# Moving the next batch's attention one step ahead in the odd batches of a fused attention and gated MLP

## Chip, cores and metric

The kernel runs on one core of one Trainium2 chip. The metric is the device time of one execution in microseconds (us). TensorE, VectorE, ScalarE, GpSimd and SyncE appear in the profile as PE (with PEld for weight loads), DVE, ACT, POOL and SP.

## The reference, cut to what matters

```python
def _attn_ref(x, state):                    # x (8, 8, 512, 64), state (8, 8, 32, 64)
    a = softmax(scale * x @ state.T)        # 512 tokens attend to 32 states
    xread = a @ state
    a2 = softmax(scale * state @ x.T)       # and the states to the tokens
    sread = a2 @ x
    return concatenate([xread, sread], axis=2)

def _moe_ref(x, w_in, w_out):               # 4352 x 512, 512 x 2048, 2048 x 512
    h = x @ w_in
    g = h * np.cos(h)
    return g @ w_out
```

(`softmax` stands for the max, exp, sum and division that the reference writes out.)

## The kernel before

Each of the 8 batches is 16 steps. A step makes one 128 x 512 tile of `h`, gates it (h cos h, with range reduction), and multiplies an older tile into the output. Between these, the attention of the *next* batch is dealt out to the steps. Batches are taken in pairs; in odd batches 3 and 5 steps 0 to 7 make `h` by a scheme with fewer products, and steps 8 to 15 by plain matmuls:

```python
hps = ctx.enter_context(tc.tile_pool(name="hps", bufs=2, space=PSUM))   # two banks for h

def hidden(t):                                   # PE, L471
    t.hp = hps.tile([P, S], F32, name="h")[:, 0:t.n]
    for i in range(t.kn):
        nc.tensor.matmul(out=t.hp, lhsT=t.lhs(i), rhs=t.rhs(i), ...)
def gate(t):   nc.scalar.activation(t.q.bitcast(I32), t.hp, func=ACTF.Copy, bias=0.25)      # L567
def gate2(t):  nc.vector.tensor_tensor(t.q, t.q.bitcast(I32), t.hp, op=ALU.subtract)        # L570
def gate3(t):  nc.scalar.activation(t.q, t.q, func=ACTF.Sin, bias=halfpi, scale=-TWO_PI)    # L573
def gate4(t):  nc.vector.tensor_tensor(t.g, t.hp, t.q, op=ALU.mult)     # L580: h's bank is free
```

(some lines of these functions are cut). The order of one step, which is the order of each engine's queue:

```python
    # ... matmuls of h
    go(0)                       # attention's matmuls of this step
    gate(t); gate2(t)           # in odd steps 0-7, gate was made in the step before
    go(1); go(3)                # x_act, x_dve: attention's ops AHEAD of gate3 and gate4
    gate3(t)
    if later: later.pop(0)()    # a sum or an output transpose (store, L651) on VectorE
    gate4(t)
    sums(t)                     # "minus", L586
    go(2); go(4)                # y_act, y_dve: attention's ops BEHIND gate4
    # ... output matmuls (L624), of a tile three steps back
```

And the plan of the attention of batch `b + 1`, with `s` the list of steps 1, 2, 5, 6, 7, 8, 9:

```python
            pe[s[2]].append((b, "scores"))
            x_dve[s[2]].append((b, "max1"))         # L333
            x_dve[s[3]].append((b, "spread1"))      # L339: into rows of xT
            y_dve[s[3]].append((b, "shift"))        # L356
            x_dve[s[4]].append((b, "max2"))         # L349
            y_act[s[4]].append((b, "exps"))         # exp1 and exp2, with a table load
            x_dve[s[5]].append((b, "sums"))         # L333, L375, L376
            y_dve[s[5]].append((b, "spread1"))      # the second spread
            x_dve[s[6]].append((b, "norm1"))        # L386: aT = z1 * spread
```

The turned weights are copied (L397, twice in step 10), and read by L409 from step 11 on.

```python
            self.spread, self.z2 = xT[:, 0:2], xT[:, 2:4]
            self.a2T = xT[:, 0:2].rearrange("p j (c m) -> p j c m", c=NC)
```

Of the kernel before, what the change touches and what calls it, by code (L numbers as in the profile page):

```python
# [21 lines left out]
def kernel(  # L22
# [813 lines left out]
    def plan(b):  # L836
        pe, x_act, y_act, x_dve, y_dve = [
            {s: [] for s in range(NF)} for _ in range(5)]

        def prod(s, b, nt, *bank):  # L840
            pe[s].append((b, "products", nt) + bank)
            if b == 1 and 0 < nt < 3:
                x_dve[s].append((b, "products_taken", nt) + bank)
            else:
                x_act[s].append((b, "products_kept", nt) + bank)

        def pairs(s, b, name, kept, i):
            pe[s] += [(b, name, i), (b, name, i + 1)]
            x_act[s].append((b, kept, i))
            y_act[s].append((b, kept, i + 1))  # L850

        def early(b, s):
            if b == 1:
                pairs(s[0], b, "tokens", "tokens_kept", 0)
                pairs(s[1], b, "tokens", "tokens_kept", 2)
            else:
                for k in range(NK):
                    to = (x_dve, y_dve)[k % 2]
                    to[s[k // 2]].append((b, "tokens_turned", k))
            pe[s[2]].append((b, "scores"))  # L860
            x_dve[s[2]].append((b, "max1"))
            x_dve[s[3]].append((b, "spread1"))
            y_dve[s[3]].append((b, "shift"))
            x_dve[s[4]].append((b, "max2"))
            y_act[s[4]].append((b, "exps"))
            x_dve[s[5]].append((b, "sums"))
            y_dve[s[5]].append((b, "spread1"))
            x_dve[s[6]].append((b, "norm1"))

        def late(b, s):  # L870
            pairs(s[0], b, "turn", "turn_kept", 0)
            pe[s[1]].append((b, "reads", 0))
            pe[s[2]].append((b, "reads", 1))
            x_dve[s[2]].append((b, "keep"))
            if len(s) > 3:
                turned(b, s[3])

        def turned(b, s):
            pe[s].append((b, "keep2"))
            x_act[s].append((b, "keep3"))  # L880


        if b == 0:
            pe[0].append((0, "products", 0, SIDE, HC, WC))
            y_dve[0] += [(0, "products_taken", 0, SIDE, HC, WC),
                         (0, "inverse2")]
            prod(7, 0, 2, SIDE)
            prod(11, 0, 3)
            prod(13, 1, 0, MAIN)
            late(0, (1, 2, 3, 4))  # L890
            early(1, (5, 6, 7, 8, 9, 10, 11))
            late(1, (12, 13, 14))
        else:
            bank = (SIDE,) if b == 1 else ()
            if b == 1:
                turned(1, 0)
            prod(0, b, 1, *[MAIN for _ in bank])
            prod(4, b, 2, *bank)
            prod(9, b, 3, *bank)
            if b + 1 < B:  # L900
                prod(13, b + 1, 0)
                early(b + 1, (1 + (b == 1), 2 + (b == 1), 5, 6, 7, 8, 9))
                late(b + 1, (10, 11, 12, 15))
        return pe, x_act, y_act, x_dve, y_dve

# [21 lines left out]
    for step, t in enumerate(all_tiles):  # L927
        s = step % NF
        if s == 0 and t.b < B:
            steps = plan(t.b)  # L930
# [119 lines left out]
```

## Time and profile before

| | before |
|---|---|
| median | 765.45 us of 3 runs (764.82 to 768.66); 765.67 of 6, the 3 made beside the changed kernel included |
| span of the profiled run | 764.2 us |
| PE busy | 751.7 us, 98% |
| PE's waits for DVE's L580 | 4.3 us in all |
| late starts of L471 in steps 10 and 11 | 0.35 and 0.95 us, in batches 3 and 5 |
| granted clock, mean | 0.997 |

TensorE is as good as always busy, so time moves only where it waits. The lines are in the prediction. A line of the order of time reads: start, duration, engine, line of the kernel, operation, what it writes and reads, shape, count, and in brackets the idle time before it and what ended that. A tile's two matmuls make four records here, 0.43 us apart.

### The profile page before, as it was taken

The page shows a single profiled execution, that of the slowest core. Times are in us where ns is not written, and L with a number is a line of the kernel's source. Part 1 is how long each engine was busy: PE and PEld are TensorE (multiplying, and loading weights), DVE is VectorE, ACT ScalarE, POOL GpSimd, SP SyncE. Part 2 cuts the span into 40 slices and gives each one's busy share as a digit, 9 for nine tenths or more (in the row PEclk, how much of TensorE's full clock was granted, in tenths as well). Part 3 has the DMA queues.
Part 4 walks back from the last instruction along what each step waited for, and adds up shares of the span by engine and source line. Part 5 has one row for each costly group of instructions (what it writes and reads, how often), then busy time and mean ns, then how long its engine had stood idle before and what let it go on. Part 6 is the DMA issues. An engine that isn't in the chain of part 4 may idle for free.

```text
span 764.2 us, 8416 instructions
## 1 busy us (share of the span) xinstructions
PE 751.7 (98%) x2880; PEld 380.4 (50%) x2880; DVE 520.3 (68%) x862; ACT 316.3 (41%) x523; POOL 249.3 (33%) x258
## 2 busy tenths in 40 slices
PE   8998999999999999999999999999999999999997
PEld 3443443445555554445555553445555554455554
DVE  5778777836896788847886789747878676432431
ACT  3887844533254335333362335333443333212212
POOL 2354278777121210662221111751211206500200
PEclk9999999999999999999999999999999999999999
DMA  8595461050002510340105210420100115000021
GB/s 247 170 274 209 131 98 29 4 107 1 14 15 49 90 28 4 54 82 0 29 1 97 41 28 15 70 54 1 27 1 1 28 28 138 0 0 15 14 42 41
DMA packets 161962, 43.54 MB, mean 57 GB/s; under 512 B 153920, under 2 KB 153920, under 8 KB 161920
## 3 DMA queue, kind: packets, MB, share of 16 engines
q1 hardware_dynamic: 161024, 42.49, 25.7%
q10 hardware_dynamic: 768, 0.39, 0.2%
q8 instruction: 23, 0.38, 0.2%
q14 instruction: 19, 0.16, 0.1%
q0 software_dynamic: 128, 0.13, 0.1%
HBM read 34.08 MB, written 8.91 MB: 56 GB/s over the span
## 4 chain that ended last, share of the span: by engine, by line
PE 87%; DVE 7%; ACT 2%; issue 1%; DMA 1%; POOL 1%; SPq 0%; DVEq 0%; ACTq 0%; POOLq 0%
PE o L624 47%; PE h L514 14%; PE h L471 14%; PE at L319 4%; PE o L744 4%; PE at L409 2%; DVE xT L339 1%; PE o L319 1%; DVE q L570 1%; DVE g_all L580 1%; DVE i L333 1%; DMA g_all<-in_moe_w_in_dram 1%; ACT q L567 1%; PE at L392 1%; DVE aT L356 1%
## 5 line engine op out<-in xcount | busy, mean ns | idle before, releaser
L624 PE MATMUL o<-g_all,w_out 128*128 128x512 f32 x512 | 236.4, 598 | 0.4 <-POOL w_out L242 0.4
L624 PE MATMUL o<-g_all,s 128*128 128x512 f32 x384 | 177.3, 598 | 0.0
L586 POOL TENSOR_TENSOR g_all<-g_all 128x512 f32<-128x512 f32 x80 | 112.8, 1433 | 121.2 <-DVE g_all L580 121.2
L624 PEld LDWEIGHTS o<-g_all,w_out 128*128 128x128 f32 x512 | 93.8, 190 | 113.1 <-issue 108.4
L573 ACT ACTIVATE q<-q,halfpi 128x512 f32<-128x512 f32 (+1 forms) x144 | 100.8, 700 | 95.8 <-DVE q L570 95.6
L624 PEld LDWEIGHTS o<-g_all,s 128*128 128x128 f32 x384 | 70.8, 190 | 88.1 <-issue 82.1
L570 DVE TENSOR_TENSOR q<-q,h 128x512 f32<-128x512 int32 (+1 forms) x69 | 42.9, 621 | 103.6 <-ACT q L567 103.6
L471 PE MATMUL h<-aT,sw 128*128 128x512 f32 x224 | 107.2, 602 | 4.8 <-DVE g_all L580 4.3
L567 ACT ACTIVATE q<-g_all 128x512 int32<-128x512 f32 x75 | 46.8, 624 | 141.8 <-DVE g_all L560 141.4
L567 ACT ACTIVATE q<-h 128x512 int32<-128x512 f32 (+1 forms) x69 | 37.6, 545 | 131.0 <-PE h L471 131.0
L570 DVE TENSOR_TENSOR q<-q,g_all 128x512 f32<-128x512 int32 x75 | 52.7, 703 | 35.5 <-ACT q L567 35.5
L471 PEld LDWEIGHTS h<-aT,sw 128*128 128x128 f32 x224 | 41.8, 190 | 60.2 <-issue 45.0
L509 POOL TENSOR_TENSOR swS<-sw 128x128 f32<-128x128 f32 x35 | 17.4, 496 | 148.6 <-PE h L514 107.3
L580 DVE TENSOR_TENSOR g_all<-g_all,q 128x512 f32<-128x512 f32 x75 | 54.0, 720 | 14.5 <-ACT q L573 14.4
L580 DVE TENSOR_TENSOR g_all<-h,q 128x512 f32<-128x512 f32 (+1 forms) x69 | 42.8, 621 | 23.5 <-ACT q L573 23.1
L242 POOL TENSOR_TENSOR w_out<-w_out,s 128x1024 int32<-128x1024 int32 x10 | 23.9, 2390 | 77.6 <-DVE w_out L237 73.4
L509 POOL TENSOR_TENSOR swS<-sw,swS 128x128 f32<-128x128 f32 x35 | 18.3, 522 | 87.4 <-PE h L514 86.9
L514 PEld LDWEIGHTS h<-aT,sw 128*128 128x128 f32 x144 | 27.4, 190 | 34.4 <-issue 28.0
L514 PE MATMUL h<-aS,sw 128*128 128x256 f32 x144 | 43.1, 381 | 0.1
L514 PE MATMUL h<-aS,swS 128*128 128x256 f32 x144 | 42.8, 379 | 0.0
L514 PE MATMUL h<-aT,sw 128*128 128x256 f32 x144 | 42.8, 379 | 0.0
L586 DVE TENSOR_TENSOR g_all<-g_all 128x512 f32<-128x512 f32 x48 | 33.5, 697 | 1.6
(107 smaller groups left out, 886.3 us busy)
## 6 DMA issues: line engine op xcount, KB each, us to landing
out_dram<-ot SPq DMA_DIRECT2D x132, 64.0 KB, 2.0
g_all<-in_moe_w_out_dram SPq DMA_DIRECT2D x8, 1024.0 KB, 5.0
g_all<-in_moe_w_in_dram SPq DMA_DIRECT2D x6, 1024.0 KB, 5.3
xT<-in_x_dram SPq DMA_DIRECT2D x96, 64.0 KB, 2.3
x_b<-in_x_dram SPq DMA_DIRECT2D x24, 256.0 KB, 4.5
x_b<-in_x_dram SPq DMA_DIRECT2D x16, 128.0 KB, 3.8
g_all<-in_moe_w_in_dram SPq DMA_DIRECT2D x4, 512.0 KB, 5.9
x_b<-in_moe_w_out_dram SPq DMA_DIRECT2D x1, 1024.0 KB, 6.1
```

Of the source, the lines that this page charges most:

```text
L242: nc.gpsimd.tensor_tensor(bits, bits, e, op=ALU.add)
L319: nc.tensor.matmul(out=(to or at)[j][Ns * k:Ns * k + Ns, 0:n], lhsT=w[D * j:D * j + D, self.b, Ns * k:Ns * k + Ns], rhs=r(slice(D * j, D * ...
L471: nc.tensor.matmul(out=t.hp, lhsT=t.lhs(i), rhs=t.rhs(i), start=(i == 0), stop=(i == t.kn - 1))
L509: engine.tensor_tensor(o, x1, x2, op=op)
L514: nc.tensor.matmul(out=out, lhsT=w, rhs=r, start=True, stop=True)
L567: nc.scalar.activation(t.q.bitcast(I32), t.hp, func=ACTF.Copy, bias=0.25)
L570: nc.vector.tensor_tensor(t.q, t.q.bitcast(I32), t.hp, op=ALU.subtract)
L573: nc.scalar.activation(t.q, t.q, func=ACTF.Sin, bias=halfpi, scale=-TWO_PI)
L580: nc.vector.tensor_tensor(t.g, t.hp, t.q, op=ALU.mult)
L586: engine.tensor_tensor(out, a, b, op=ALU.subtract)
L624: nc.tensor.matmul(out=acc[bank][ch], lhsT=w[:, i, P * ch:P * ch + P], rhs=g.g, start=(i == 0), stop=(i == NH - 1))
L744: nc.tensor.matmul(out=acc[MAIN][i], lhsT=t.g[:, P * i:P * i + P], rhs=w_out[:, :, t.f, :], start=(t.n_th == 0), stop=(t.n_th == NF - 1))
```

## The change

Its intent is to take the next batch's attention out of steps 8 and 9, where TensorE's steps are short and VectorE's long, by doing it a step sooner. The small product (`prod`) has to leave step 4, whose two PSUM banks the scores now take.

```diff
-            prod(4, b, 2, *bank)
+
+            soon = int(b % 2 == 1 and b > 1)
+            prod(4 - soon, b, 2, *bank)
             prod(9, b, 3, *bank)
             if b + 1 < B:
                 prod(13, b + 1, 0)
-                early(b + 1, (1 + (b == 1), 2 + (b == 1), 5, 6, 7, 8, 9))
+                early(b + 1, (1 + (b == 1), 2 + (b == 1)) + tuple(
+                    s - soon for s in (5, 6, 7, 8, 9)))
                 late(b + 1, (10, 11, 12, 15))
```

## The prediction

> **What bounds the kernel now.** I read the page first, then TensorE's waits, then the order of time on each engine around the two places where TensorE waits in batch 3.
>
> ```profile
> PE 751.7 (98%) x2880; PEld 380.4 (50%) x2880; DVE 520.3 (68%) x862; ACT 316.3 (41%) x523; POOL 249.3 (33%) x258
> ...
> PE h L471 <- DVE g_all L580: 4.3, 6, 1.9
> ```
>
> TensorE is busy 751.7 of 764.2 us. Whatever the change does, it pays only through TensorE's waits, and most of what it still waits for in mid-kernel is the last gating multiply on VectorE (L580), which frees one of the two PSUM banks `h`. TensorE in order of time, batch 3, steps 8 to 11:
>
> ```profile
> 296.52 1.88 PE L471 MATMUL h<-aT,sw 128*128 128x512 f32 x4
> 298.24 1.88 PE L624 MATMUL o<-g_all,s 128*128 128x512 f32 x4
> 299.95 1.88 PE L471 MATMUL h<-aT,sw 128*128 128x512 f32 x4
> 301.76 1.09 PE L319 MATMUL at<-w_in,st_all 64*32 64x512 f32 x16
> 302.78 1.98 PE L624 MATMUL o<-g_all,s 128*128 128x512 f32 x4
> 304.95 1.98 PE L471 MATMUL h<-aT,sw 128*128 128x512 f32 x4 [0.18 <-DVE g_all L580]
> 306.77 1.04 PE L392 MATMUL at<-ident,xT 128*128 128x128 f32 x8
> 307.65 1.88 PE L624 MATMUL o<-g_all,s 128*128 128x512 f32 x4
> 310.32 1.98 PE L471 MATMUL h<-aT,sw 128*128 128x512 f32 x4 [0.79 <-DVE g_all L580]
> ```
>
> L471 opens steps 8, 9, 10 and 11. Matmul ends are modelled, so I use starts: step 8 without a wait is 299.95 - 296.52 = 3.43 us. A set of small products costs 1.22 more: even step 4 with it runs from 277.75 to 283.70, 5.95 us, and the same step 6 without it from 288.36 to 293.09, 4.73. So step 10 was due at 299.95 + 3.43 + 1.22 = 304.60 and came 0.35 late. Step 11 was due at 306.77 + 0.88 (turn) + 1.72 (output) = 309.37 and came 0.95 late. Batch 5 repeats both (472.24 and 477.61). All that the change can win is therefore 2 x (0.35 + 0.95) = 2.6 us, 0.34%.
>
> VectorE over the same stretch:
>
> ```profile
> 297.56 0.69 DVE L580 TENSOR_TENSOR g_all<-g_all,q 128x512 f32<-128x512 f32 x1
> 298.28 0.69 DVE L586 TENSOR_TENSOR g_all<-g_all 128x512 f32<-128x512 f32 x1
> 298.89 1.28 DVE L630 SCALAR_TENSOR_TENSOR held<-o,held 128x512 f32<-128x512 f32 x2
> 301.23 0.69 DVE L570 TENSOR_TENSOR q<-q,h 128x512 f32<-128x512 int32 x1 [1.06 <-ACT q L567]
> 301.83 1.30 DVE L333 TRANSPOSE_TENSOR_REDUCE i<-aT 128x16 f32<-128x512 f32 x2
> ...
> 304.25 0.65 DVE L580 TENSOR_TENSOR g_all<-h,q 128x512 f32<-128x512 f32 x1
> ...
> 305.54 1.24 DVE L339 STREAM_TRANSPOSE xT<-i 128x1024 f32<-128x1024 f32 x1
> ...
> 307.27 1.79 DVE L386 TENSOR_TENSOR aT<-aT,xT 128x1024 f32<-128x1024 f32 x1
> ```
>
> L580 at 304.25 is step 8's, and step 10's matmul starts 0.70 us after it. Before it stand step 8's sums (L333); *behind* it stand the spread (L339) and norm (L386) of the next batch. The 1.06 us of idle is ScalarE's: it does the exponentials from 297.02 to 300.60, both table loads around them, and takes step 8's first gate op only then.
>
> **What the Trainium skill says.** "TensorE: Matmul & The Clock Gate", Architectural detail, says ACT and DVE are "strict FIFO"; every order seen here agrees, so the order of the program decides. "ScalarE: Activation LUTs", What ACT_TABLE_LOAD costs, gives about 1283 ns a load; the loads at 297.02 and 301.21 took 1.28 us each. "GPSIMD Engine Reference", Specifications, says POOL shares SBUF interfaces with VectorE when an instruction has two SBUF inputs; L386 has a median of 1231 ns over its eight runs but took 1.79 us at 307.27, with POOL at work. The same TensorE page, Part 1, says that a free-running window of about 3.4 us with an idle array halves the clock for the next. The trace has one case: TensorE idle 1.95 us before 73.03, then
>
> ```profile
> 71.00:73.00 2.00, 0.09 (x1) 0.00 (x0) 1.95 (x3) 1.99 (x5) 0.48 (x1) 1.00 0.05 19
> 73.00:76.00 3.00, 2.97 (x4) 0.84 (x4) 1.90 (x3) 2.97 (x5) 1.87 (x1) 0.62 0.77 245
> ```
>
> (granted clock 0.62, third column from the end). Against the usual spacing the starts after 73.57 lost 0.29 + 0.42 + 0.47 + 0.40 = 1.6 us, about half of one window. The 0.95 waits did not trigger it (1.00).
>
> **The change, part by part.** No instruction is added or removed; it all lies in the order of queues. In batches 3 and 5 scores and max go from step 5 to 4, spread and shift to 5, max2 and exponentials to 6, sums and second spread to 7, norm to 8; the small product goes from step 4 to 3 (in batch 7 that alone, which I count as 0: the two copies behind it fit where ScalarE idles).
>
> TensorE does the same sum of work. Step 4 starts 1.22 later (278.97), step 5 too, step 6 as before at 288.36. I replay the in-order queues from there with the durations of the trace, start to start where ops stand back to back.
>
> Names: gate is ScalarE's L567, gate2 L570, sine L573, gate4 L580, minus L586; max L333, spread L339, shift L356, max2 L349 (with L351), sums L333 to L376, norm L386, store L651. In an even step L559 and L560 come first and gate waits for L560.
>
> - Step 4, VectorE: L560 at 278.97 + 1.49 = 280.46 (the same delay as at 259.97), gate2 1.45 later (281.91; that chain through ScalarE is as at 279.85 to 281.28). Then 0.61 gate2, 1.23 max, 0.62 store, 0.68 gate4, 0.61 minus: 285.66.
> - Step 5: gate2 0.61, wait 0.1, three adds 1.58, spread 1.16, gate4 0.69, minus 0.61, shift 1.20: 291.6. TensorE needs the adds by 288.36 and they end at 288.0.
> - Step 6: two adds to L560 at 292.0; gate2 at 293.45; 0.61, max2 1.40, gate4 0.70, minus 0.61: 296.8. ScalarE: sine 294.15, step 7's gate 294.8 to 295.4, then the exponentials with their table 295.4 to 299.0, then the sine table to 300.3.
> - Step 7: gate2 to 297.4; sums wait for exp1 (297.75) and end 299.6; gate4 waits for the sine, now *behind* the exponentials (300.35 to 301.07), so VectorE idles 1.4 and gate4 starts at 301.1. Then 0.72, minus 0.61, spread 1.16, L630 1.20: 304.8.
> - Step 8: gate2 0.61, norm 1.22 (POOL is idle there), store 0.65: gate4 at 307.3, against 304.25.
>
> So step 8's gate4 has spread and norm, 1.16 + 1.22 us, in front of it that stood behind it, and ScalarE's idle is not saved but moved a step earlier and is longer (1.4 for 1.06). Step 10's matmuls start at 307.3 + 0.70 = 308.0, 3.4 late instead of 0.35. Step 9's gate4 then comes at about 310.1, so step 11 no longer waits: 308.0 + 4.42 (step 10's length, 309.37 - 304.95) = 312.4, against 310.32. Loss 2.1 us a batch. Later steps have next to no waits that could take it back. Two batches: 4.2 us.
>
> Then the clock. An idle of 3.4 us leaves at least 1.6 us in one window wherever the window falls; here, if windows fall as now, about 2.2 us from 305.8. I put 0.85 on a halved window, at 1.65 us each: 2 x 0.85 x 1.65 = 2.8 us.
>
> Sum: 765.45 + 4.2 + 2.8 = 772.4.
>
> **Rivals.** (a) It works as meant: exponentials off step 8 let its gate op start 1.7 us sooner, and both waits go. For it: the 1.06 of VectorE idle before 301.23. Against: from 285 to 299 VectorE has hardly any idle, so it can't absorb work earlier. This makes 762.9 at best. (b) The waits only change places, with VectorE's total work before step 9's gate4 being the same in both: about 765 to 766. Against: the output of steps 8 to 10 is short (1.72 us), so a late step 10 leaves no room before step 11. (c) The loss without the clock: 769.7, if neither batch crosses into half rate. (d) Another wait, step 6's for step 5's adds (0.3 us of room): up to 1 us a batch more.
>
> **Range and chances.** (c) to (d) with both halvings span 769.7 to 775; an error of a microsecond a batch in the replay, or a run of before that is itself 0.5 high, opens the low side to 767. The range is 767.0 to 775.0. Faster by over 2% is impossible by the 2.6 us limit; slower by 2% would need 15 us.
>
> **What would show it.** Right: gate4 of step 8 near 307 with L339 and L386 ahead of it; an idle of some 3 us before L471 near 308 and 477, no wait before the next; a VectorE idle of over 1 us before the gate4 near 301, behind the table load; a window with granted clock under 1 after each wait. Wrong: gate4 of step 8 before 305, a total of TensorE waits below that of before, or a wait in steps 5 to 7 in place of step 10.

## The result and the profile after

The changed kernel took 772.53 us, median of 6 runs (771.24 to 773.3), against 765.67 for the kernel before. The ratio is 1.0083, 95% interval 1.0064 to 1.0103: slower by 0.8%, clear of noise. Ratios and intervals here are from fast runs of the same rounds; they are not quite the ratio of the medians. All outputs are right.

The page's line of busy times and the largest of TensorE's waits, kernel after:

```profile
PE 754.4 (98%) x2880; PEld 382.3 (50%) x2880; DVE 520.0 (67%) x862; ACT 317.2 (41%) x523; POOL 248.1 (32%) x258
...
PE h L471 <- DVE g_all L580: 8.5, 4, 3.1
```

TensorE's waits for L580 have doubled in sum, from 4.3 to 8.5 us, in 4 places instead of 6. Those that the change was to shorten, in batches 3 and 5, went from 2 x (0.18 + 0.79) = 1.9 to 2 x 3.08 = 6.2. TensorE in order of time, steps 8 to 11 of batch 3:

```profile
296.80 1.88 PE L471 MATMUL h<-aT,sw 128*128 128x512 f32 x4
...
303.06 1.98 PE L624 MATMUL o<-g_all,s 128*128 128x512 f32 x4
308.12 3.07 PE L471 MATMUL h<-aT,sw 128*128 128x512 f32 x4 [3.08 <-DVE g_all L580]
310.99 1.68 PE L392 MATMUL at<-ident,xT 128*128 128x128 f32 x8
312.51 1.88 PE L624 MATMUL o<-g_all,s 128*128 128x512 f32 x4
314.23 1.88 PE L471 MATMUL h<-aT,sw 128*128 128x512 f32 x4
```

Step 8 starts at 296.80, 0.28 later than before, which comes from the first microseconds of the run. Step 10 was due at 296.80 + 8.08 = 304.88 and starts 3.24 late. Step 11 then has no wait, but step 10 took 308.12 to 314.23, 6.11 us instead of 4.42: the L471 group shows why, 3.07 us for what took 1.98 before. In these traces the granted clock changes only at borders that lie a multiple of 3.413 us apart; one such stretch is called a window here. Two windows (columns: busy time and count of PE, PEld, DVE, ACT, POOL; then clock, DMA share, GB/s):

```profile
308.88:312.29 3.41, 3.41 (x10) 1.87 (x9) 2.99 (x5) 1.52 (x3) 3.41 (x3) 0.50 0.68 108
479.55:482.96 3.41, 3.41 (x9) 1.76 (x8) 2.83 (x6) 1.32 (x2) 3.41 (x3) 0.50 0.68 107
```

Both are at 0.50, the first in batch 3 and the second in batch 5, and each follows the window that holds most of the wait. VectorE shows where step 8's gate4 went:

```profile
301.40 0.69 DVE L580 TENSOR_TENSOR g_all<-g_all,q 128x512 f32<-128x512 f32 x1 [1.38 <-ACT q L573]
302.13 0.69 DVE L586 TENSOR_TENSOR g_all<-g_all 128x512 f32<-128x512 f32 x1
302.74 1.24 DVE L339 STREAM_TRANSPOSE xT<-i 128x1024 f32<-128x1024 f32 x1
303.90 1.25 DVE L630 SCALAR_TENSOR_TENSOR held<-o,held 128x512 f32<-128x512 f32 x2
305.07 0.67 DVE L570 TENSOR_TENSOR q<-q,h 128x512 f32<-128x512 int32 x1
305.67 1.21 DVE L386 TENSOR_TENSOR aT<-aT,xT 128x1024 f32<-128x1024 f32 x1
306.80 0.70 DVE L651 STREAM_TRANSPOSE ot<-held 128x512 f32<-128x512 f32 x1
307.42 0.65 DVE L580 TENSOR_TENSOR g_all<-h,q 128x512 f32<-128x512 f32 x1
```

The L580 at 307.42 is the one that stood at 304.25. L339 and L386, which followed it before, are now ahead of it. The idle of 1.38 us at the top is ScalarE's exponentials and their two table loads, which the sine of step 7 now queues behind:

```profile
295.65 1.28 ACT L360 ACT_TABLE_LOAD   x1
296.94 1.06 ACT L360 ACTIVATE aT<-aT 128x1024 f32<-128x1024 f32 x1
...
299.35 1.28 ACT L573 ACT_TABLE_LOAD   x1
300.65 0.72 ACT L573 ACTIVATE q<-q,halfpi 128x512 f32<-128x512 f32 x1
```

**Where the 7 us went.** Step 11 starts 314.23 - 296.80 = 17.43 us after step 8, before 310.32 - 296.52 = 13.80. That is 3.63 us in batch 3, of which 6.11 - 4.42 = 1.69 are the halved clock and the remaining 1.94 are the wait (3.24, less the 0.35 + 0.95 that went). Batch 5 repeats it (467.62 to 485.05 against 463.82 to 477.61). Twice 3.63 is 7.3; the tails below differ by 7.0, the stretches after each step 11 being some 0.1 us shorter.

### The profile page after: what moved, and what is told of

Read it like the earlier page. It is cut to its first block, busy times and chain, and to the rows that moved or that the text cites. A ratio compares the mean times of both kernels' runs of the same rounds, so it can differ in the third digit from the quotient of the medians.

```text
span 771.5 us, 8414 instructions
## 1 busy us (share of the span) xinstructions
PE 754.4 (98%) x2880; PEld 382.3 (50%) x2880; DVE 520.0 (67%) x862; ACT 317.2 (41%) x523; POOL 248.1 (32%) x258
## 4 chain that ended last, share of the span: by engine, by line
PE 87%; DVE 6%; ACT 3%; issue 1%; DMA 1%; POOL 1%; SPq 0%; DVEq 0%; ACTq 0%; POOLq 0%
PE o L624 47%; PE h L471 14%; PE h L514 14%; PE at L319 4%; PE o L744 4%; PE at L409 2%; PE at L392 1%; DVE xT L339 1%; PE o L319 1%; DVE g_all L580 1%; DMA g_all<-in_moe_w_in_dram 1%; ACT q L567 1%; DVE q L570 1%; DVE aT L356 1%; ACT q L573 0%
## 5 line engine op out<-in xcount | busy, mean ns | idle before, releaser
L471 PE MATMUL h<-aT,sw 128*128 128x512 f32 x224 | 109.8, 615 | 9.0 <-DVE g_all L580 8.5
L471 PEld LDWEIGHTS h<-aT,sw 128*128 128x128 f32 x224 | 42.6, 193 | 64.4 <-issue 45.5
L580 DVE TENSOR_TENSOR g_all<-g_all,q 128x512 f32<-128x512 f32 x75 | 53.9, 719 | 16.5 <-ACT q L573 16.4
L580 DVE TENSOR_TENSOR g_all<-h,q 128x512 f32<-128x512 f32 (+1 forms) x69 | 42.9, 621 | 24.2 <-ACT q L573 23.8
```

Source lines behind the costliest of these rows:

```text
L471: nc.tensor.matmul(out=t.hp, lhsT=t.lhs(i), rhs=t.rhs(i), start=(i == 0), stop=(i == t.kn - 1))
```

## The experiments

The start of a run varies by 1 to 3 us from execution to execution, with the clock of its first 80 us: step 8 of batch 3 starts at 295.15 to 295.87 us in the six traces in which the clock was never halved by then, and at 296.52 to 298.13 in the eight in which it was, once. So beside the time I give the *tail*: from the start of step 8's L471 in batch 3 to the end of the span. It holds both disputed places, in batches 3 and 5 (tails are from the trace's unrounded times). Before it is 764.2 - 296.5 = 467.7, after it is 771.5 - 296.8 = 474.7. Each median is of 4 to 6 runs, each tail of one profiled run. The waits are those shown in the profile in batch 3, in brackets before L471 unless L409 is named; "half" counts windows at half clock in batches 3 and 5.

| run | median us | ratio to before (95%) | tail us | waits, batch 3 | half |
|---|---|---|---|---|---|
| before | 765.67 | | 467.7 | 0.18, 0.79 | 0 |
| after | 772.53 | 1.0083 (1.0064 to 1.0103) | 474.7 | 3.08 | 2 |
| e1 product only | 766.13 | 1.0004 (0.9990 to 1.0018) | 467.7 | 0.18, 0.79 | 0 |
| e2 norm behind | 770.59 | 1.0061 (1.0047 to 1.0074) | 472.0 | 2.24, 0.43 | 1 |
| e3 both behind | 768.75 | 1.0038 (1.0024 to 1.0052) | 470.1 | 1.12, L409 1.24 | 0 |
| e4 first half | 767.56 | 1.0030 (1.0016 to 1.0043) | 470.0 | 1.19, 0.79 | 0 |
| e5 order only | 771.6 | 1.0078 (1.0065 to 1.0092) | 472.4 | 2.77 | 1 |
| e6 gates first | 773.74 | 1.0102 (1.0088 to 1.0115) | 475.2 | 0.48, L409 2.83 | 2 |
| e7 norm only | 766.09 | 1.0005 (0.9992 to 1.0017) | 468.1 | 0.18, L409 1.23 | 0 |
| e8 wait filled | 769.67 | 1.0052 (1.0036 to 1.0067) | 471.3 | none before L471 | 0 |
| e9 store behind | 763.36 | 0.9972 (0.9960 to 0.9984) | 465.3 | none | 0 |
| e10 norm, other buffer | 765.34 | 1.0001 (0.9989 to 1.0013) | 466.4 | 0.17 | 0 |
| e11 e9 and conversions | 762.5 | 0.9965 (0.9954 to 0.9977) | 465.3 | none | 0 |
| e12 e3, other buffer | 765.39 | 1.0005 (0.9992 to 1.0018) | 468.3 | 1.10 | 0 |

The theory is that the loss comes from the *place* of spread and norm ahead of step 8's gate4 in VectorE's queue, and from the half clock that the wait brings. Rivals: R1, doing the first half of the attention sooner costs by itself; R2, the exponentials ahead of step 7's sine on ScalarE are the cost; R3, the small product's new place.

### e1: the product alone

```diff
-            prod(4, b, 2, *bank)
+            prod(4 - int(b % 2 == 1 and b > 1), b, 2, *bank)
```

> Only the small product goes from step 4 to step 3 in batches 3, 5 and 7; the attention stays. Theory (the loss is the place of spread and norm ahead of step 8's gate4 in VectorE's queue): the time of before, 765.7 us, within 0.5, with the two waits of 0.3 and 0.9 us before L471 in batches 3 and 5 as before. Rival R3 (the product's new place costs): 768 to 772 us.

766.13 us, and the same two waits to the hundredth. R3 falls, and batch 7, where the product alone moves, is free too.

### e5: the order alone

The kernel before, with spread and norm directly behind the sums in step 8.

```diff
-            y_dve[s[5]].append((b, "spread1"))
-            x_dve[s[6]].append((b, "norm1"))
+            (x_dve if b in (4, 6) else y_dve)[s[5]].append((b, "spread1"))
+            x_dve[s[6] - (b in (4, 6))].append((b, "norm1"))
```

> The kernel before, nothing sooner, but the second spread and the norm stand directly behind the sums in step 8, so ahead of step 8's gate4. Theory (place in the queue, not the earlier step): gate4 of step 8 near 306.6 instead of 304.25, TensorE waits 2.6 us before step 10 and not before step 11, 1.4 us lost a batch: 768.6 us, up to 771.9 if the wait halves the clock in both. Rivals R1 (an earlier first half) and R2 (the exponentials ahead of the sine): both untouched here, so 765.7 us.

771.6 us, most of the loss of the change, with the exponentials untouched and nothing but the norm in an earlier step (8 instead of 9, which is its place in the change). VectorE in order of time, step 8, which started at 296.93:

```profile
304.19 1.25 DVE L339 STREAM_TRANSPOSE xT<-i 128x1024 f32<-128x1024 f32 x1
305.47 1.22 DVE L386 TENSOR_TENSOR aT<-aT,xT 128x1024 f32<-128x1024 f32 x1
306.62 0.70 DVE L651 STREAM_TRANSPOSE ot<-held 128x512 f32<-128x512 f32 x1
307.24 0.65 DVE L580 TENSOR_TENSOR g_all<-h,q 128x512 f32<-128x512 f32 x1
```

Gate4 comes 10.31 us after the step's start, before 304.25 - 296.52 = 7.73, after 307.42 - 296.80 = 10.62. So the two ops in front of it are enough. From step 8 to step 11 this run takes 312.36 - 296.93 = 15.43 us, 1.63 more than before; of the 3.63 of the change, 1.94 were the wait. The order alone thus brings 1.63 of 1.94 us a batch, and a half window in batch 5 besides.

### e2, e3, e12: everything sooner, but norm, or spread and norm, behind the gate

e2 puts only the norm behind gate4, in step 8:

```diff
-            x_dve[s[6]].append((b, "norm1"))
+            (y_dve if b in (4, 6) else x_dve)[s[6]].append((b, "norm1"))
```

> The changed kernel, but in batches 3 and 5 the norm of step 8 stands behind gate4 and minus in VectorE's queue, nothing else. Theory: gate4 of step 8 near 306.3 instead of 307.4, the wait of TensorE about 2 us instead of 3.1, step 11 about 1 us sooner a batch, so 770.4 us with both half-rate windows and down to 767 without them; I expect 769. Rival R2 (the loss is ScalarE's, the exponentials and their table ahead of step 7's sine): ScalarE's order is untouched, so 772.5 us.

The wait fell from 3.08 to 2.24 us and gate4 came 9.74 us after the step's start instead of 10.62. The time, 770.59, is just over the upper end of what was expected (770.4), and its interval overlaps that of the change, so here it is the wait that tells, not the time. One of the two windows was still at half clock, and the norm, now beside GpSimd's own subtractions, took 2.29 us instead of 1.21, so that step 11 got a wait of 0.43. The trace gives the size of that: in before, e2 and e10 the norm ends 1.08 us after the end of the subtraction that GpSimd was at when it started (307.99 to 309.07, 309.04 to 310.12, 310.96 to 312.04).

e3 puts both behind, in steps 8 and 9:

```diff
-            y_dve[s[5]].append((b, "spread1"))
-            x_dve[s[6]].append((b, "norm1"))
+            y_dve[s[5] + (b in (4, 6))].append((b, "spread1"))
+            (y_dve if b in (4, 6) else x_dve)[s[6] + (b in (4, 6))].append(
+                (b, "norm1"))
```

> The changed kernel, but spread goes back to step 8 and norm to step 9, both behind that step's gate4 and minus; all else as sooner as in the change, exponentials included. Theory: gate4 of step 8 near 305.1, TensorE waits some 0.9 us before step 10 and not before step 11, no half-rate window: 764.8 us, slightly under before. Rival R2: 770 to 772.5 us, since the exponentials still stand ahead of step 7's sine.

768.75 us, a miss by 4: the wait before step 10 is down to 1.12, near the 0.9 expected, but a new one of 1.24 us stands before L409. R2, which expected 770 or more, does not fit either. The cause showed in e7 below: the norm has a second customer. e12 is e3 with the second spread in another buffer, `aS`, that is idle then, so that nobody waits to overwrite it:

```diff
+        def second_spread(self):
+            if self.b in (4, 6):
+                self.spread = aS.rearrange("p (j h) s -> p j (h s)", j=2)
+            self.spread1()
...
-            y_dve[s[5] + (b in (4, 6))].append((b, "spread1"))
+            y_dve[s[5] + (b in (4, 6))].append((b, "second_spread"))
```

> e3 once more (everything up to the sums a step sooner, spread and norm behind gate4 of steps 8 and 9) with the second spread in aS. Corrected theory: the wait of 1.24 us before L409 goes, that of 1.1 before step 10 stays, 2.4 us less than e3: 766.3 us, the time of before, so the sooner exponentials and sums are worth nothing by themselves. If not the shared rows: 768.7 us as e3.

765.39 us: the wait before L409 is gone and the kernel is as fast as before, with scores, exponentials and sums a step sooner. TensorE in order of time (line numbers as in e10 below: L476 is L471, L585 is L580 and L414 is L409):

```profile
304.62 1.98 PE L476 MATMUL h<-aT,sw 128*128 128x512 f32 x4 [1.10 <-DVE g_all L585]
309.04 1.88 PE L476 MATMUL h<-aT,sw 128*128 128x512 f32 x4
310.85 1.09 PE L414 MATMUL at<-x_b,xT 128*64 128x128 f32 x16
```

R2 falls as an explanation of the whole: with the exponentials where the change puts them, the tail is 468.3 us, 0.6 over before. But sooner attention is not free. e10 below differs from e12 in the sooner part alone, and its tail is 1.9 us shorter (466.4); the medians, 765.34 and 765.39, don't tell the two apart. In e12 this cost is set off by the norm, which no longer stands ahead of step 9's gate4.

### e4: the first half alone

Scores, max, first spread, shift and max2 a step sooner; exponentials, sums and norm where they were (the edit: `soon` is taken from steps 5, 6 and 7 only, and `exps` goes to `y_act[s[4] + soon]`).

> The kernel before, with only scores, max, first spread, shift and max2 (and the product) one step sooner in batches 3 and 5; exponentials stay in step 7, sums in 8, norm in 9. Theory in its full form (VectorE has no idle in steps 4 to 7, so work put there delays the gates of steps 6 and 7, hence the exponentials and step 8's gate): gate4 of step 8 near 305.7, waits of 1.5 and 1.1 us a batch, about 768.3 us. Rival R2 (only the exponentials' new place costs): 765.7 us or less.

767.56 us. R1 is true in part: sooner work in steps 4 to 7 delays what follows on VectorE. Gate4 of step 8 comes 304.03 - 295.15 = 8.88 us after the step's start instead of 7.73, though nothing new stands in that step. The delay is passed through ScalarE: VectorE waits 1.58 us for step 8's first gate op (1.06 before), which queues behind exponentials that start later (their table load 296.80 - 295.15 = 1.65 us after the step's start, 0.50 before):

```profile
301.02 0.69 DVE L570 TENSOR_TENSOR q<-q,h 128x512 f32<-128x512 int32 x1 [1.58 <-ACT q L567]
304.03 0.65 DVE L580 TENSOR_TENSOR g_all<-h,q 128x512 f32<-128x512 f32 x1
```

This costs 2.4 us of tail, against 7.0 for the change.

### e8: matmuls in the wait

The changed kernel with three useless matmuls into a free PSUM bank at the end of step 9, in TensorE's queue ahead of step 10's:

```diff
+        if t.b in (3, 5) and s == 9:
+            for _ in range(3):
+                nc.tensor.matmul(out=acc[SIDE][1], lhsT=ident,
+                                 rhs=w_in[:, 0, 0:S], start=True, stop=True)
```

> The changed kernel with three useless matmuls of 0.86 us each in TensorE's queue ahead of step 10's, into a PSUM bank that is free then (its last reader is L630 at 303.9 to 305.1), so that they run inside the wait. Theory (some 3 us of the loss are half-rate windows that the idle brings): granted clock 1.00 in batches 3 and 5 and 1.6 us less a batch, 769.3 us, though 5 us of matmuls were added. Rival (the idle alone is the loss): 772.5 us or more.

Over the order of time and the clock (same columns as above):

```profile
303.83 2.84 PE L1023 MATMUL o<-w_in,ident 128*128 128x512 f32 x6 [0.16 <-DVE held L630]
306.75 1.98 PE L471 MATMUL h<-aT,sw 128*128 128x512 f32 x4
...
308.00:312.00 4.00, 4.00 (x16) 2.16 (x15) 3.01 (x6) 2.83 (x5) 4.00 (x4) 1.00 0.65 103
```

The matmuls fill the wait, step 10 still starts when gate4 lets it (11.33 us after step 8, 11.32 in the changed kernel), and the clock stays at 1.00. The tail is 471.3 us, 3.4 less than the changed kernel's: the price of two half-rate windows, apart from the waits.

### e7, e6, e10: what the norm's second customer is

These start from the kernel before and look for a version that beats both. e7 puts the norm behind gate4 of step 9 (the edit of e2), e6 also the sums behind gate4 of step 8 and the spread behind gate4 of step 9.

> The kernel before, with only the norm of batches 3 and 5 behind gate4 and minus of step 9. Theory: the wait of 0.95 us before step 11 goes, that of 0.35 before step 10 stays: 763.8 us. If the wait only moves: 765.7 us.

> The kernel before, with sums and norm of batches 3 and 5 behind gate4 and minus of their steps (8 and 9) and the second spread behind those of step 9. Theory: gate4 of step 8 near 303.3 and of step 9 near 308, both early enough, so both waits go: 2 x 1.3 us less, 763.1 us, under both kernels. If the waits only move to step 12 because the attention ends later: 765 to 766 us.

Both missed, e6 by over 10 us. e7's TensorE and ScalarE in order of time:

```profile
308.70 1.88 PE L471 MATMUL h<-aT,sw 128*128 128x512 f32 x4
311.82 1.09 PE L409 MATMUL at<-x_b,xT 128*64 128x128 f32 x16 [1.23 <-ACT xT L397]
...
311.18 0.59 ACT L397 COPY xT<-at 128x512 f32<-128x512 f32 x1 [3.25 <-PE h L471]
```

Step 11's wait for gate4 is gone (308.70 is on time), but the reads L409 wait for the copy L397, and L397 starts 0.1 us after the norm's end (308.82 + 2.29 = 311.11). The bracket names L471 as what ended its wait, but that group had ended at 308.70 + 1.88 = 310.58. In the code L397 writes the rows of `xT` that the norm reads. e10 tests that: e7 with the second spread in `aS`, as in e12.

> e7 once more, but the second spread of batches 3 and 5 is written to aS, which nobody reads between steps 6 and 11, instead of rows of xT. Corrected theory for e3, e6 and e7 (the copy of the turned weights, L397, overwrites the spread in xT, so it waits for the norm, and the reads L409 wait for the copy): the waits of 1.24 us before L409 go, that before step 10 of 0.2 stays: 763.8 us. If the copy waited for something else: 766.1 us as e7.

The wait before L409 is gone; TensorE, ScalarE and VectorE in order of time, e10 (its line numbers are 5 higher below the inserted method, so L476 is L471, L414 is L409, L402 is L397 and L391 is L386):

```profile
309.64 1.88 PE L476 MATMUL h<-aT,sw 128*128 128x512 f32 x4
311.45 1.09 PE L414 MATMUL at<-x_b,xT 128*64 128x128 f32 x16
...
308.77 0.57 ACT L402 COPY xT<-at 128x512 f32<-128x512 f32 x1
...
309.75 2.29 DVE L391 TENSOR_TENSOR aT<-aT,aS 128x1024 f32<-128x1024 f32 x1
```

The copy now starts before the norm. So the mechanism of e3 and e7 is the shared rows (e12 and e10 show it). For e6 it is read from the order alone: its L397 starts at 313.74, after the norm's end at 311.42 + 2.24 = 313.66. The time is a miss, though: 765.34 us, no gain by the ratio. The tail is 1.2 us shorter than before, not 1.9: step 11 takes 316.47 - 309.64 = 6.83 us instead of 6.47. Its second product needs an accumulator whose halves ScalarE's L640 and VectorE's L642 empty, the latter behind the norm. They end at 314.37 and 315.45, and the matmuls into the halves start at 314.42 and 315.50. That this is the 0.36 is argued from these times; no run moves the two ops. In e6, sums, spread and norm together make L409 wait 2.83 us and halve the clock in both batches.

### e9 and e11: something else behind the gate

What can wait is the output transpose L651. e9 is the kernel before with the two of steps 8 and 9 behind gate4 and minus of steps 9 and 10:

```diff
-        if later:
+        behind = t.b in (3, 5) and s in (8, 9, 10)
+        if later and not behind:
             later.pop(0)()
...
         if t.pair is not None:
             sums(t)
+        if later and behind and s > 8:
+            later.pop(0)()
```

> The kernel before; in batches 3 and 5 the two output transposes (L651, 0.62 us each) of steps 8 and 9 go behind gate4 and minus of steps 9 and 10. The norm stays where it was, so nothing that the turned weights' copy into the same rows of xT waits for comes later. Theory: gate4 of step 8 near 303.6 and of step 9 near 308.4, the wait before step 10 gone, that before step 11 under 0.1 us: 2.4 us less than before, 763.3 us, under both kernels. If some other wait takes over again: 765.7 us.

763.36 us, ratio 0.9972 (0.9960 to 0.9984), as expected: 2.4 us of tail, and no wait in brackets any more:

```profile
306.21 1.88 PE L471 MATMUL h<-aT,sw 128*128 128x512 f32 x4
307.93 1.04 PE L392 MATMUL at<-ident,xT 128*128 128x128 f32 x8
308.80 1.88 PE L624 MATMUL o<-g_all,s 128*128 128x512 f32 x4
310.72 1.98 PE L471 MATMUL h<-aT,sw 128*128 128x512 f32 x4
```

Step 8 started at 298.13 here, so step 10 is on time at 298.13 + 8.08 = 306.21. This version beats both kernels. e11 adds the same idea in batch 0, where two conversions stood ahead of step 9's gate4:

```diff
-            elif last >= 0:
+            elif last >= 0 and step != 9:
                 convert(last, "bcdf")
...
+        if step == 9 and last >= 0:
+            convert(last, "bcdf")
```

> e9, and in batch 0 the two conversions (L234, L237, 1.9 us) of step 9 behind that step's gate4. There TensorE waits 1.95 us before 73.03 and then runs a window at half rate (1.6 us). Theory: this wait goes, no half-rate window near 74, but the next gate4 (behind the sums, near 76.5) makes step 12 wait about 1 us: 2.5 us less than e9, 760.8 us.

762.5 us. The wait of 1.95 us in batch 0 is gone, and the next gate4 makes TensorE wait 0.68 and later 0.40 us. Less came of it than expected, at least in part because the half clock after that wait falls only in some executions anyway: in 6 of the 13 traces that have this wait. Its interval overlaps that of e9, so e11 is not shown to be faster than e9.

## Why the prediction was right

- **Which wait.** It said that step 8's gate4 would come at 307.3 with L339 and L386 ahead of it. It came at 307.42, in a run 0.28 later from the start, so 307.14 by the prediction's clock. e5 shows that this order alone brings most of the loss, e12 that with both ops behind gate4, and the rows no longer shared, the kernel is as fast as before.
- **VectorE's idle.** 1.4 us before step 7's gate4, behind exponentials and table load: 1.38 in the profile. One reading of the kernel before was loose: it put both table loads ahead of step 8's first gate op, but the second, at 301.21, comes after that op, at 300.60. The replay of the change has them right.
- **The wait and the loss.** 3.4 late and 2.1 us lost a batch: 3.24 late and 1.94 lost.
- **The clock.** 1.65 us for a halved window, at 0.85 each: 1.69 measured, and both came in the profiled run. e8 took them away and won 3.4 us. Of the six timed runs three have a mean clock of 0.992 or 0.993 (772.91 to 773.3 us) and three of 0.996 (771.24 to 772.16). So not all executions pay for the same number of windows, which the 0.85 allowed for. The bar of 1.6 us of idle in one window was set too low, however. Counted back from e2's halved window of batch 5, which starts at 477.4, in steps of 3.413 us, a border falls at 306.8 in batch 3; e2's wait there, 305.0 to 307.24, lies 1.8 us in one window, and the next was not halved. Counted in this way over all 14 traces, after their first 15 us, each of the 12 windows with 1.94 to 2.83 us of idle was followed by one at half clock, and none with 1.93 us or less. With that bar a wait of 3.08 us escapes if a border falls 1.14 to 1.94 us after its start, 0.80 of 3.41 us; if borders fall anywhere alike, that makes an estimate of 0.77 a window where the prediction had 0.85. That the sum then met the median within 0.2 us, with the six runs spread over 2, is partly luck.
- **Rivals.** (a) fell. (b) fell, though its premise held: step 9's gate4 came at 310.18, or 309.90 by the prediction's clock, against 309.62 before. But TensorE's step 10 is too short to make up for its late start. (c) was refuted by the clock, (d) by the absence of any wait in steps 5 to 7: step 5's adds ended at 287.64 + 0.69 = 288.33 and step 6 started at 288.64.
- **What it did not see.** It treated the norm as having no consumer before step 11. It has one in step 10, through the shared rows of `xT`. That did not touch the prediction, since the norm comes sooner there, but it spoiled my expectations of e3, e6 and e7.

## What to carry to other kernels

When an engine's queue is full, "sooner" only decides what stands in front of what: look for the op that frees a buffer for the bottleneck engine, and put behind it what nobody waits for. Before putting an op behind, list everyone who waits for it, including those who wait to overwrite what it reads. A wait on TensorE that grows past some 2 us can cost nearly as much again in clock: here 1.69 us beside 1.94 in each batch.

## What the Trainium skill lacked or had wrong

- "TensorE: Matmul & The Clock Gate", Why this matters for your kernels: warns of idle gaps over about 3 us. Here shorter ones did it: waits of 1.95 us (before), 2.24 (e2, batch 5) and 2.77 (e5, batch 5) were each followed by a window at 0.50, while 2.24 and 2.77 in batch 3 of the same runs were not. How much of the wait falls in one window decides: in these traces 1.94 us of idle or more halved the next, 1.93 or less didn't.
- "ScalarE: Activation LUTs", What ACT_TABLE_LOAD costs: adds about 1380 ns of drain to a load's 1283. Here the exponential of the kernel after started 1.29 us after its load (295.65 to 296.94), and the whole switch cost that.
